# Loading q and k of later tiles in 32x32 blocks and transposing them on VectorE, in a chunked attention with a low-rank mixer and an MLP

## The chip, the cores and the metric

The kernel runs on one core of a Trainium2 chip. The metric is the device time of one execution in microseconds (us), the median of several runs; less is better. Engine names are those of the profile: PE is TensorE's matmul, PEld its weight load, DVE is VectorE, ACT is ScalarE, POOL is GpSimd, SP is SyncE. SP computes nothing here: it issues nearly all DMAs, one after the other. A row with "SPq" is such an issue.

## What is computed

The inputs are q, k and v of 8 batches, 8 heads, 576 rows and 64 columns, and the weights of a mixer (U, V) and of an MLP (w_ch1, w_ch2, 512 to 2048 to 512).

```python
def _attn_ref(q, k, v):                       # chunk = 64, nc = 9
    scores = scale * np.matmul(q_c, k_c.transpose(0, 1, 2, 4, 3))   # 64x64 a chunk and head
    scores = scores - np.max(scores, axis=-1, keepdims=True)
    attn = np.exp(scores)
    attn = attn / (np.sum(attn, axis=-1, keepdims=True) + 1e-09)
    return np.matmul(attn, v_c)               # back to B, H, S, D

def _moe_ref(x, U, V, w_ch1, w_ch2):          # x is batch, 576, 512
    h = x.transpose(0, 2, 1) @ U @ V          # rank 32, along the sequence
    u = x + h.transpose(0, 2, 1)
    return u + np.maximum(u @ w_ch1, 0.0) @ w_ch2
```

## The kernel before

**Tiling.** Batches are taken in four pairs (pair 0 to 3). The 1152 rows of a pair make nine tiles of 128 rows, written (pair, tile); tile 4 spans both batches. Three tiles make a group, so a pair has groups 0, 1 and 2.

**MLP.** For each group and each of the 16 blocks `f` of 128 hidden columns, `hidden` does twelve PE matmuls into `h` (L567; high and low parts of the data and the weights), ACT writes `hh` (`relu_high`, L575), DVE writes `hl` (`relu_low`, L580), and `project_out` does nine PE matmuls into three `o` banks (L593). These are 192 blocks. The `o` matmuls of a block stand on PE behind the `h` matmuls of the next one, so a block's `hh` and `hl` have the time of one set of `h` matmuls to become ready.

**Attention of a tile** (`attention_ops`). SP loads `qn`, `kn` and `vn` (`load_qk` L348 and L349, `load_v` L358). PE transposes q and k, four 128x128 blocks each, into a PSUM bank (`transpose`, L375); ACT copies the bank to SBUF as `qT_` and `kT_` (`evacuate`, L385). PE makes 32 small score matmuls for the tile's 64x64 blocks (L393), DVE takes maxima and subtracts (L407, L411), ACT exponentiates (L415), PE transposes the result (`eT_`) and multiplies with v (L424), DVE divides (L436 to L442). The tile's result `x` goes through the projection `y` (L495, L496), the low-rank addition (L523, L529), a transpose into `uth` and `utl` (L535 to L548), and then feeds the MLP of its group.

**Early and later tiles.** The nine tiles of pair 0 are "early" (`early`, L327): their q, k and v live in the weights' buffers, and the change leaves them alone. The 27 tiles of pairs 1 to 3 are later ones. Their `qn`, `kn`, `vn`, `qT_`, `kT_`, `ex`, `eT_` come from a pool of eight buffers of 128x512 (`slot`, L69); the SP issue that fills such a buffer waits until the work that last used it is done, and SP waits with it.

**Order.** The first part (pair 0's attention, the conversion of the weights, 32 MLP blocks, and tiles (1, 0) and (1, 1)) is put in order by a list planner written in the kernel (`order`, L124), from a cost in us, an engine and the buffers that each `Op` takes and frees. After that, `plan` (L744) hands the steps of attention, projection and mixing out evenly over the 16 blocks of a group: `attend` (L718) has for each tile a step that loads the next tile, then q, k, scores, and the transposed weights and values of the tile before. The framework's scheduler then fixes the row of instructions of each engine. Each engine works through its row strictly in order; a waiting instruction holds up all behind it. Every DMA on SP also waits for the landing of the DMA eight before it, since eight semaphores are used in turn.

Of the kernel before, what the change touches and what calls it, by code (L numbers as in the profile page):

```python
# [10 lines left out]
F32 = mybir.dt.float32  # L11
# [10 lines left out]
def kernel(  # L22
# [11 lines left out]
    nc = tc.nc  # L34
    B, H, S, D = q.shape
# [4 lines left out]
    P = 128  # L40
    C = 64
    D1 = D + 1
    HP = H // 2
    NCC = DM // P
    NF = DF // P
# [5 lines left out]
    XROOM = 3  # L51
    BLOCKS = [(hp, e, c) for hp in range(HP) for e in range(2) for c in range(2)]
    GN = GT * P
# [12 lines left out]
    def bank(name):  # L66
        return psum.tile([P, 512], F32, tag="bank", name=name)

    def slot(dtype, name, shape=(P, 512)):  # L69
        return work.tile(list(shape), dtype, tag="slot", name=name, bufs=NS)  # L70
# [33 lines left out]
    def wslot(shape, dtype, name):  # L104
        return wpool.tile([P, *shape], dtype, tag="w", name=name, bufs=NF)
# [214 lines left out]
    def segments(pr, t):  # L320
        lo, hi = t * P, (t + 1) * P
        for e in range(2):
            a, z = max(lo, e * S), min(hi, (e + 1) * S)
            if a < z:
                yield a - lo, z - a, 2 * pr + e, a - e * S

    def early(pr, t):  # L327
        return pr == 0 and t < NEARLY

    loaded = {}  # L330
    begun = {}
# [4 lines left out]
    def load_qk(pr, t):  # L336
        n = f"{pr}_{t}"
        if early(pr, t):
            words = wslot((4 * DM,), F32, "qkv_" + n)
            qn, kn = (words[:, z * DM : (z + 1) * DM].rearrange("p (h d) -> p h d", h=H) for z in range(2))  # L340
            vn = words[:, 2 * DM : 2 * DM + H * D1].rearrange("p (c a k) -> p c a k", c=2, k=D1)
        else:
            qn = slot(F32, "qn_" + n, (P, H, D))
            kn = slot(F32, "kn_" + n, (P, H, D))
            vn = slot(F32, "vn_" + n, (P, 2, HP, D1))
        nc.gpsimd.memset(vn[:, :, :, D:], 1.0)
        for r, m, b, s0 in segments(pr, t):
            nc.sync.dma_start(qn[r : r + m], q[b, :, s0 : s0 + m, :].rearrange("h s d -> s h d"))  # L348
            nc.sync.dma_start(kn[r : r + m], k[b, :, s0 : s0 + m, :].rearrange("h s d -> s h d"))  # L349
        loaded[pr, t] = qn, kn, vn  # L350

    def load_v(pr, t):
        vn = loaded[pr, t][2]
        for c in range(2):
            b, s0 = divmod(t * P + c * C, S)
            b += 2 * pr
            for e in range(2):
                (nc.gpsimd if early(pr, t) else nc.sync).dma_start(  # L358
                    vn[e * C : (e + 1) * C, c, :, 0:D],
                    v[b, e::2, s0 : s0 + C, :].rearrange("h s d -> s h d"),  # L360
                )

    def load(pr, t):
        load_qk(pr, t)
        load_v(pr, t)

    def attention_ops(pr, t, after=None):
        n = f"{pr}_{t}"
        st = {}
        mine = early(pr, t)  # L370

        def transpose(src, name):
            ps = st[name] = bank("ps_" + name + n)
            for j in range(4):
                nc.tensor.transpose(ps[:, j * P : (j + 1) * P], src[:, j * P : (j + 1) * P], ident)  # L375

        def evacuate(name):
            if name[0] == "e" or not mine:
                dst = slot(F32, name + n, (P, HP, P))
            elif name[0] == "q":  # L380
                st["qk"] = wslot((2, HP, P), F32, "qkT_" + n)
                dst = st["qk"][:, 0]
            else:
                dst = st["qk"][:, 1]
            nc.scalar.copy(dst.rearrange("p a b -> p (a b)"), st[name])  # L385
            st[name] = dst

        def scores():
            ps = [bank(f"sc{e}_{n}") for e in range(2)]
            for hp, e, c in BLOCKS:  # L390
# [8 lines left out]
                )  # L399
            st["sc"] = [p[:, 0 : HP * C].rearrange("p (h k) -> p h k", k=C) for p in ps]  # L400

        def maximum(e):
            if e == 0:
                st["ex"] = slot(F32, "ex_" + n, (P, HP, 2, C))
                st["mx"] = work.tile([P, 2, HP], F32, tag="mx", name="mx_" + n, bufs=2)
            mx = st["mx"][:, e, :]
            nc.vector.reduce_max(mx, st["sc"][e], axis=AX.X)  # L407

        def subtract(e):
            mx = st["mx"][:, e, :]  # L410
            nc.vector.tensor_sub(st["ex"][:, :, e, :], st["sc"][e], mx.unsqueeze(2).broadcast_to([P, HP, C]))  # L411
# [5 lines left out]
        def values():  # L417
# [3 lines left out]
            for hp, e, c in BLOCKS:  # L421
                rows = slice(e * C, (e + 1) * C)
                cs = slice(c * C, (c + 1) * C)
                nc.tensor.matmul(  # L424
                    ps[e][cs, hp * D1 : (hp + 1) * D1],
                    lhsT=st["eT_"][rows, hp, cs],
# [3 lines left out]
                )  # L430
            st["av"] = [p[:, 0 : HP * D1].rearrange("p (h k) -> p h k", k=D1) for p in ps]

# [6 lines left out]
        def scaled(e):  # L439
            if e == 0:  # L440
                st["x"] = work.tile([P, HP, 2, D], F32, tag="x", name="x_" + n, bufs=NX)
            nc.vector.tensor_mul(  # L442
                st["x"][:, :, e, :],
                st["av"][e][:, :, 0:D],
                st["sm"][:, e].unsqueeze(2).broadcast_to([P, HP, D]),
            )
            if e == 1:
                x_of[pr, t] = st["x"].rearrange("p a b k -> p (a b k)")

        src = lambda z: loaded[pr, t][z].rearrange("p h d -> p (h d)")  # L450
        flat = lambda: st["ex"].rearrange("p a b k -> p (a b k)")
        lq = Op("SP", 2.5, lambda: load_qk(pr, t), after, take="w" if mine else "slot slot slot", lat=2.2)
        lv = Op("POOL" if mine else "SP", 4.0 if mine else 2.5, lambda: load_v(pr, t), lq, lat=2.2)
        tq = Op("PE", 0.35, lambda: transpose(src(0), "qT_"), lq, begun.get((pr, t - 2)), take="bank")
        cq = Op("ACT", 0.58, lambda: evacuate("qT_"), tq, take="w" if mine else "slot", free="bank")
        tk = Op("PE", 0.35, lambda: transpose(src(1), "kT_"), lq, tq, take="bank")
        ck = Op("ACT", 0.58, lambda: evacuate("kT_"), tk, cq, take="" if mine else "slot", free="bank")
        sc = Op("PE", 0.62, scores, ck, take="bank bank", free="w" if mine else "slot slot slot slot")
        m0 = Op("DVE", 0.41, lambda: maximum(0), sc, take="slot mx")
        s0 = Op("DVE", 0.41, lambda: subtract(0), m0, free="bank")  # L460
        m1 = Op("DVE", 0.41, lambda: maximum(1), s0)
        s1 = Op("DVE", 0.41, lambda: subtract(1), m1, free="bank mx")
        ex = Op("ACT", 0.63, exp, s1)
        te = Op("PE", 0.35, lambda: transpose(flat(), "eT_"), ex, take="bank", free="slot")
        ce = Op("ACT", 0.58, lambda: evacuate("eT_"), te, take="slot", free="bank")
        av = Op("PE", 0.65, values, ce, lv, take="bank bank x", free="slot w" if mine else "slot slot")
        sm = Op("DVE", 0.5, sums, av, take="sm")
        x0 = Op("DVE", 0.415, lambda: scaled(0), sm, free="bank")
        x1 = Op("DVE", 0.415, lambda: scaled(1), x0, free="bank sm")
        begun[pr, t] = te  # L470
        return [[lq, lv], [tq, cq], [tk, ck], [sc, m0, s0, m1, s1, ex], [te, ce], [av, sm, x0, x1]]

    ybank = {}

# [182 lines left out]
    for item in LEAD.split():  # L657
        rank[0] += 1
        z, i = item[0], int(item[1:] or 0)
        if z == "U":  # L660
            u_done = u_ops()
        elif z == "V":
            v_done = v_ops()
        elif z == "W":
            w_done[i] = w_ops(i, w_done[i - 3][-1] if i > 2 else None)
        elif z == "T":
            xs[i] = attention_ops(0, i)[-1][-1]
        elif z == "P":
            ys[i] = project_ops(0, i, xs)[1]
        else:  # L670
            if i == 2:
                rank[0] = 0
            for t in range(GT * i, GT * i + GT):
                m = mix_ops(0, t, xs[t], ys, first=his.get(i))[1]
                his.setdefault(i, m[1])
                mixed.setdefault(i, []).append(m[2])
# [3 lines left out]
    for g, f0, f1 in STRETCHES:  # L680
        for f in range(f0, f1):
            rank[0] = BASE
            prev = block_ops(0, g, f, f == f0, f == f1 - 1, [*w_done[f], *mixed[g]], prev)
            blocks += 1
            if blocks in gates:
                rank[0] = 0
                attention_ops(1, gates[blocks], prev[0])
# [117 lines left out]
```

## Time and profile before

| | |
|---|---|
| median of 3 runs | 1030.82 us (1030.47 to 1032.12) |
| profiled execution, first to last instruction | 1032.0 us |
| ACT busy | 260.8 us (25%) |
| matmuls of the MLP: L567, L593 | 2304 and 1728 |
| SP issues of q and k of later tiles | 30 and 30, 256 KB each, 128 KB for tile 4 |
| SP issues of v of later tiles | 108, 64 KB each |

The profiled execution's span, 1032.0 us, is its own time; it is 1.2 us over the median. A matmul's "mean ns" is longer than the pace at which matmuls follow each other, since they are pipelined: the start times in the timeline tell the pace. In the source view, a row's three numbers are the shortest, the median and the longest duration in ns.

### The profile page before, as it was taken

The numbers are of one execution on the slowest core, as the hardware profiler recorded it, in microseconds if no ns is written. First come the engines' busy times: TensorE is split into PE (matmuls) and PEld (weight loads), VectorE is DVE, ScalarE is ACT, GpSimd is POOL, SyncE is SP. The second block draws the span as 40 slices with busy tenths as digits, with TensorE's granted clock in tenths as the row PEclk, the third lists the DMA queues.
The fourth block names the chain that finished last, engine by engine and source line by source line (L and its number), as shares of the span: only waits on it lengthen the run. The fifth ranks groups of instructions, "written<-read, shape, count | busy, mean of one in ns | idle before, by whom it ended". The sixth has DMA issues, their size and how long they took to land.

```text
span 1032.0 us, 16637 instructions
## 1 busy us (share of the span) xinstructions
PE 980.7 (95%) x7032; PEld 862.0 (84%) x7032; DVE 419.5 (41%) x834; ACT 260.8 (25%) x467; POOL 26.4 (3%) x78
## 2 busy tenths in 40 slices
PE   5486999999999999999999999999999999999998
PEld 4364888888888888988888888988888889999997
DVE  3498999973333342322423242322333332211211
ACT  3453234322322222222222222222222231111110
POOL 7100000000000000000000000000000000000000
PEclk9667899999999999999999999999999999999999
DMA  9952142305121211021021210111121000000000
GB/s 187 217 184 88 42 113 82 103 34 129 34 63 31 63 31 32 34 55 37 32 62 32 62 32 10 53 34 43 48 53 41 31 1 1 31 1 1 31 1 30
DMA packets 123157, 56.40 MB, mean 55 GB/s; under 512 B 107276, under 2 KB 115724, under 8 KB 123084
## 3 DMA queue, kind: packets, MB, share of 16 engines
q1 hardware_dynamic: 121932, 52.99, 20.1%
q0 software_dynamic: 1152, 2.36, 1.2%
q8 instruction: 55, 0.90, 0.4%
q14 instruction: 18, 0.15, 0.0%
HBM read 45.83 MB, written 9.51 MB: 54 GB/s over the span
## 4 chain that ended last, share of the span: by engine, by line
PE 69%; DVE 0%; ACT 0%; DVEq 0%; issue 0%; ACTq 0%
PE h L567 30%; PE o L593 30%; PE av L424 1%; PE sc L393 1%; PE ut L535 1%; PE ps_eT L375 1%; PE ps_kT L375 1%; PE ps_qT L375 1%; PE u L523 1%; PE y L496 1%; PE y L495 1%; DVE x L605 0%; DVE ex L411 0%; ACT ex L415 0%; DVEq L800 0%; DVE mx L407 0%
## 5 line engine op out<-in xcount | busy, mean ns | idle before, releaser
L567 PE MATMUL h<-uth,w 128*128 128x384 f32 x1536 | 427.1, 342 | 4.9 <-ACT w L308 2.1
L593 PE MATMUL o<-w,hh 128*128 128x512 f32 x1152 | 364.3, 403 | 0.6 <-ACT hh L575 0.6
L567 PEld LDWEIGHTS h<-uth,w 128*128 128x128 f32 x1536 | 282.4, 189 | 13.8 <-ACT w L308 2.6
L580 DVE SCALAR_TENSOR_TENSOR hl<-h,hh 128x384 fp32r<-128x384 f32 x192 | 106.8, 556 | 430.4 <-ACT hh L575 430.4
L567 PE MATMUL h<-utl,w 128*128 128x384 f32 x768 | 260.2, 339 | 0.4 <-DVE utl L548 0.4
L593 PEld LDWEIGHTS o<-w,hh 128*128 128x128 f32 x1152 | 207.8, 189 | 35.8 <-ACT hh L575 0.9
L593 PE MATMUL o<-w,hl 128*128 128x512 f32 x576 | 217.9, 395 | 0.0
L575 ACT ACTIVATE hh<-h 128x384 fp32r<-128x384 f32 x192 | 94.3, 491 | 477.3 <-PE h L567 477.2
L567 PEld LDWEIGHTS h<-utl,w 128*128 128x128 f32 x768 | 144.9, 189 | 6.6 <-DVE utl L548 0.6
L593 PEld LDWEIGHTS o<-w,hl 128*128 128x128 f32 x576 | 108.2, 188 | 25.0 <-DVE hl L580 0.3
L375 PE MATMUL ps_eT<-ident,ex 128*128 128x128 f32 x144 | 24.8, 301 | 25.0 <-ACT ex L415 25.0
L415 ACT ACTIVATE ex<-ex 128x512 f32<-128x512 f32 x36 | 22.7, 632 | 89.7 <-DVE ex L411 89.1
L375 PEld LDWEIGHTS ps_eT<-ident,ex 128*128 128x128 f32 x144 | 18.9, 153 | 31.1 <-ACT ex L415 27.9
L407 DVE TENSOR_REDUCE mx<-sc 128x4 f32<-128x256 f32 x72 | 28.0, 418 | 37.7 <-PE sc L393 37.7
L488 DVE TENSOR_TENSOR xl<-x,xh 128x512 fp32r<-128x512 f32 x40 | 27.2, 687 | 29.6 <-ACT xh L484 25.6
L529 DVE TENSOR_TENSOR x<-u,x 128x512 f32<-128x512 f32 x36 | 24.1, 684 | 26.7 <-PE u L523 26.4
L548 DVE TENSOR_TENSOR utl<-ut,uth 128x512 fp32r<-128x512 f32 x36 | 24.5, 690 | 25.2 <-ACT uth L543 25.1
L605 DVE TENSOR_TENSOR x<-o,x 128x512 f32<-128x512 f32 x48 | 31.2, 685 | 7.7 <-PE o L593 7.6
L543 ACT CAST uth<-ut 128x512 fp32r<-128x512 f32 x36 | 20.9, 587 | 40.4 <-PE ut L535 36.6
L385 ACT COPY eT<-ps_eT 128x512 f32<-128x512 f32 x36 | 21.1, 586 | 39.4 <-PE ps_eT L375 39.4
L484 ACT CAST xh<-x 128x512 fp32r<-128x512 f32 x40 | 24.1, 621 | 17.8 <-PE y L496 7.5
L411 DVE TENSOR_TENSOR ex<-sc,mx 128x256 f32<-128x256 f32 x72 | 28.0, 417 | 0.8
(74 smaller groups left out, 590.2 us busy)
## 6 DMA issues: line engine op xcount, KB each, us to landing
wraw<-in_moe_w_ch_dram SPq DMA_DIRECT2D x32, 512.0 KB, 4.5
out_dram<-x SPq DMA_DIRECT2D x36, 256.0 KB, 2.1
vn<-in_v_dram SPq DMA_DIRECT2D x108, 64.0 KB, 2.9
qn<-in_q_dram SPq DMA_DIRECT2D x24, 256.0 KB, 3.3
kn<-in_k_dram SPq DMA_DIRECT2D x24, 256.0 KB, 4.1
qkv<-in_v_dram POOLq DMA_DIRECT2D x36, 64.0 KB, 6.3
qkv<-in_q_dram SPq DMA_DIRECT2D x8, 256.0 KB, 9.4
qkv<-in_k_dram SPq DMA_DIRECT2D x8, 256.0 KB, 7.6
```

The lines of the kernel that those rows point to most:

```text
L375: nc.tensor.transpose(ps[:, j * P : (j + 1) * P], src[:, j * P : (j + 1) * P], ident)
L407: nc.vector.reduce_max(mx, st["sc"][e], axis=AX.X)
L411: nc.vector.tensor_sub(st["ex"][:, :, e, :], st["sc"][e], mx.unsqueeze(2).broadcast_to([P, HP, C]))
L484: nc.scalar.copy(st["h"], x_of[pr, i + 4 * e])
L488: nc.vector.tensor_sub(st["l"], x_of[pr, i + 4 * e], st["h"])
L529: nc.vector.tensor_add(x, st["u"], x)
L548: nc.vector.tensor_sub(ul[:, :, js], st["t"].rearrange("p (c t) -> p c t", c=NCC), uh[:, :, js])
L567: nc.tensor.matmul(ps[:, :GN], lhsT=w[:, z, cc], rhs=u[:, cc, :], start=(n == 0), stop=(n == 3 * NCC - 1))
L575: nc.scalar.activation(hh, ps[:, :GN], AF.Relu)
L580: nc.vector.scalar_tensor_tensor(hl, ps[:, :GN], 0.0, hh, op0=ALU.max, op1=ALU.subtract)
L593: nc.tensor.matmul(acc[j], lhsT=h[:, js], rhs=w2[f][:, z], start=(first and i == 0), stop=(final and i == 2),)
L605: nc.vector.tensor_add(x, ps, x)
```

## The change

Tiles of pairs 1 to 3 are loaded and transposed in another way. `qn` and `kn` become buffers of 128 partitions x 4 head pairs x 4 blocks x 32 columns. For each of q and k a tile is fetched by 16 DMAs (in tile 4, eight for each of its two halves): each brings one block of 32 rows and 32 of the 64 columns, for the four even or the four odd heads, to 32 partitions. That is 128 pieces of 128 bytes a DMA, 16 KB; before, it was one DMA of 128 rows and 8 heads, 1024 pieces of 256 bytes. One DVE instruction over the 128x512 buffer then transposes every 32x32 block and writes `qT_` or `kT_`, which have the layout that the scores read before. The eight PE transposes, the two PSUM banks and the two ACT copies of such a tile go away. The planner's costs for (1, 0) and (1, 1) have 0.6 us on DVE for each transpose.

```diff
+    TB = 32
...
-            qn = slot(F32, "qn_" + n, (P, H, D))
-            kn = slot(F32, "kn_" + n, (P, H, D))
+            qn = slot(F32, "qn_" + n, (P, HP, 4, TB))
+            kn = slot(F32, "kn_" + n, (P, HP, 4, TB))
...
         for r, m, b, s0 in segments(pr, t):
-            nc.sync.dma_start(qn[r : r + m], q[b, :, s0 : s0 + m, :].rearrange("h s d -> s h d"))
-            nc.sync.dma_start(kn[r : r + m], k[b, :, s0 : s0 + m, :].rearrange("h s d -> s h d"))
+            for dst, src in ((qn, q), (kn, k)):
+                if early(pr, t):
+                    nc.sync.dma_start(dst[r : r + m], src[b, :, s0 : s0 + m, :].rearrange("h s d -> s h d"))
+                    continue
+                for z in range(4):
+                    e, j = divmod(z, 2)
+                    for i in range(m // TB):
+                        s1 = s0 + i * TB
+                        nc.sync.dma_start(
+                            dst[z * TB : (z + 1) * TB, :, r // TB + i, :],
+                            src[b, e::2, s1 : s1 + TB, j * TB : (j + 1) * TB].rearrange("h t d -> t h d"),
+                        )
...
+        def turned(z, name):
+            dst = slot(F32, name + n, (P, HP, P))
+            nc.vector.transpose(dst.rearrange("p a b -> p (a b)"), loaded[pr, t][z].rearrange("p a i d -> p (a i d)"))
+            st[name] = dst
...
-        tq = Op("PE", 0.35, lambda: transpose(src(0), "qT_"), lq, begun.get((pr, t - 2)), take="bank")
-        cq = Op("ACT", 0.58, lambda: evacuate("qT_"), tq, take="w" if mine else "slot", free="bank")
-        tk = Op("PE", 0.35, lambda: transpose(src(1), "kT_"), lq, tq, take="bank")
-        ck = Op("ACT", 0.58, lambda: evacuate("kT_"), tk, cq, take="" if mine else "slot", free="bank")
+        if mine:
...
+        else:
+            cq = Op("DVE", 0.6, lambda: turned(0, "qT_"), lq, begun.get((pr, t - 2)), take="slot")
+            ck = Op("DVE", 0.6, lambda: turned(1, "kT_"), cq, take="slot")
+            turns = [[cq], [ck]]
...
-        return [[lq, lv], [tq, cq], [tk, ck], [sc, m0, s0, m1, s1, ex], [te, ce], [av, sm, x0, x1]]
+        return [[lq, lv], *turns, [sc, m0, s0, m1, s1, ex], [te, ce], [av, sm, x0, x1]]
```

Line numbers of the changed kernel are larger by one in its first part and by 22 in its last; the rows below have them as they are. The first two numbers in a name are pair and tile.

The row of SP before, from the loads of (1, 5) to those of (1, 7):

```order
L358 DMA vn_1_5_2516<-in_v_dram 64x4x64
L348 DMA qn_1_5_2514<-in_q_dram 128x8x64
L349 DMA kn_1_5_2515<-in_k_dram 128x8x64
L358 DMA vn_1_5_2516<-in_v_dram 64x4x64 x3
L358 DMA vn_1_6_2787<-in_v_dram 64x4x64
L348 DMA qn_1_6_2785<-in_q_dram 128x8x64
L358 DMA vn_1_6_2787<-in_v_dram 64x4x64
L349 DMA kn_1_6_2786<-in_k_dram 128x8x64
L358 DMA vn_1_6_2787<-in_v_dram 64x4x64 x2
L358 DMA vn_1_7_2868<-in_v_dram 64x4x64
L348 DMA qn_1_7_2866<-in_q_dram 128x8x64
```

and the same stretch of SP now:

```order
L357 DMA qn_1_5_2622<-in_q_dram 32x4x32 x16
L357 DMA kn_1_5_2623<-in_k_dram 32x4x32 x16
L369 DMA vn_1_5_2624<-in_v_dram 64x4x64 x4
L369 DMA vn_1_6_2915<-in_v_dram 64x4x64
L357 DMA qn_1_6_2913<-in_q_dram 32x4x32 x16
L357 DMA kn_1_6_2914<-in_k_dram 32x4x32 x16
L369 DMA vn_1_6_2915<-in_v_dram 64x4x64 x3
L357 DMA qn_1_7_3014<-in_q_dram 32x4x32 x16
L357 DMA kn_1_7_3015<-in_k_dram 32x4x32 x16
```

A tile's six issues are now 36, in the same queue and nearly the same sequence.

DVE before, at the end of group 2 of pair 0 (`hl_0_2_13` to `hl_0_2_15` belong to the last three blocks of that group; `x` is the low-rank addition, `utl` the low part of the next group's data):

```order
L580 SCALAR_TENSOR_TENSOR hl_0_2_13_3081<-h_0_2_13_3066,hh_0_2_13_3079 128x384
L529 TENSOR_TENSOR x_1_2_2463<-u_1_2_3095,x_1_2_2463 128x512
L548 TENSOR_TENSOR utl_1_0_3089<-ut_1_0_3083,uth_1_0_3088 128x4x128
L548 TENSOR_TENSOR utl_1_0_3089<-ut_1_1_3104,uth_1_0_3088 128x4x128
L580 SCALAR_TENSOR_TENSOR hl_0_2_14_3126<-h_0_2_14_3111,hh_0_2_14_3124 128x384
L548 TENSOR_TENSOR utl_1_0_3089<-ut_1_2_3128,uth_1_0_3088 128x4x128
L580 SCALAR_TENSOR_TENSOR hl_0_2_15_3159<-h_0_2_15_3144,hh_0_2_15_3157 128x384
```

and DVE there now:

```order
L602 SCALAR_TENSOR_TENSOR hl_0_2_13_3249<-h_0_2_13_3234,hh_0_2_13_3247 128x384
L463 STREAM_TRANSPOSE qT_1_7_3405<-qn_1_7_3014 128x512
L551 TENSOR_TENSOR x_1_2_2571<-u_1_2_3263,x_1_2_2571 128x512
L463 STREAM_TRANSPOSE kT_1_7_3429<-kn_1_7_3015 128x512
L570 TENSOR_TENSOR utl_1_0_3257<-ut_1_0_3251,uth_1_0_3256 128x4x128
L570 TENSOR_TENSOR utl_1_0_3257<-ut_1_1_3272,uth_1_0_3256 128x4x128
L602 SCALAR_TENSOR_TENSOR hl_0_2_14_3294<-h_0_2_14_3279,hh_0_2_14_3292 128x384
```

Both transposes of (1, 7) stand ahead of `hl_0_2_14`. Before, the PE transposes of that tile stood behind the `o` matmuls that read `hl_0_2_14`.

DVE before, where tile (1, 0) is transposed among the conversions of the weights (`wroom`, `wraw`, `w`):

```order
L101 TENSOR_TENSOR wroom_9_1410<-wroom_9_1410,wraw_9_1341 128x1024
L92 TENSOR_SCALAR wroom_10_1496<-wroom_10_1496 128x1024
L93 TENSOR_SCALAR wroom_10_1496<-wroom_10_1496 128x1024
L311 TENSOR_TENSOR w_9_1528<-wroom_9_1410,w_9_1528 128x1024
L580 SCALAR_TENSOR_TENSOR hl_0_1_6_1550<-h_0_1_6_1514,hh_0_1_6_1541 128x384
```

and now:

```order
L102 TENSOR_TENSOR wroom_9_1410<-wroom_9_1410,wraw_9_1341 128x1024
L93 TENSOR_SCALAR wroom_10_1526<-wroom_10_1526 128x1024
L463 STREAM_TRANSPOSE qT_1_0_1564<-qn_1_0_1488 128x512
L463 STREAM_TRANSPOSE kT_1_0_1566<-kn_1_0_1489 128x512
L312 TENSOR_TENSOR w_9_1558<-wroom_9_1410,w_9_1558 128x1024
L602 SCALAR_TENSOR_TENSOR hl_0_1_6_1584<-h_0_1_6_1544,hh_0_1_6_1581 128x384
```

The two transposes come in front of the last step of the weights of block 9 and of `hl_0_1_6`.

More of the change, by code (lines that the diff above doesn't have):

```diff
@@ L453, in attention_ops @@
         lv = Op("POOL" if mine else "SP", 4.0 if mine else 2.5, lambda: load_v(pr, t), lq, lat=2.2)
-        tq = Op("PE", 0.35, lambda: transpose(src(0), "qT_"), lq, begun.get((pr, t - 2)), take="bank")
-        cq = Op("ACT", 0.58, lambda: evacuate("qT_"), tq, take="w" if mine else "slot", free="bank")
-        tk = Op("PE", 0.35, lambda: transpose(src(1), "kT_"), lq, tq, take="bank")
-        ck = Op("ACT", 0.58, lambda: evacuate("kT_"), tk, cq, take="" if mine else "slot", free="bank")
+        if mine:
+            tq = Op("PE", 0.35, lambda: transpose(src(0), "qT_"), lq, begun.get((pr, t - 2)), take="bank")
+            cq = Op("ACT", 0.58, lambda: evacuate("qT_"), tq, take="w", free="bank")
+            tk = Op("PE", 0.35, lambda: transpose(src(1), "kT_"), lq, tq, take="bank")
+            ck = Op("ACT", 0.58, lambda: evacuate("kT_"), tk, cq, free="bank")
+            turns = [[tq, cq], [tk, ck]]
+        else:
+            cq = Op("DVE", 0.6, lambda: turned(0, "qT_"), lq, begun.get((pr, t - 2)), take="slot")
+            ck = Op("DVE", 0.6, lambda: turned(1, "kT_"), cq, take="slot")
+            turns = [[cq], [ck]]
         sc = Op("PE", 0.62, scores, ck, take="bank bank", free="w" if mine else "slot slot slot slot")
```

## The prediction, made before the changed kernel was run

> **What bounds the kernel now.** I read the page's busy shares and slices first, then the timeline of PE, then the groups by line.
>
> ```profile
> PE 980.7 (95%) x7032; PEld 862.0 (84%) x7032; DVE 419.5 (41%) x834; ACT 260.8 (25%) x467; POOL 26.4 (3%) x78
> PE   5486999999999999999999999999999999999998
> PEclk9667899999999999999999999999999999999999
> ```
>
> PE is full from about a tenth of the span on. Its pace shows in the start times: first a block of the MLP with nothing beside it, then one with both transposes of a tile.
>
> ```profile
> 1000.06 0.34 PE L567 MATMUL h<-utl,w 128*128 128x384 f32 x1
> ...
> 1004.27 0.34 PE L567 MATMUL h<-utl,w 128*128 128x384 f32 x1
> ```
>
> ```profile
> 521.22 0.34 PE L567 MATMUL h<-uth,w 128*128 128x384 f32 x1
> ...
> 523.33 0.61 PE L375 MATMUL ps_qT<-ident,qn 128*128 128x128 f32 x4
> ...
> 525.17 0.60 PE L375 MATMUL ps_kT<-ident,kn 128*128 128x128 f32 x4
> ...
> 526.32 0.34 PE L567 MATMUL h<-uth,w 128*128 128x384 f32 x1
> ```
>
> The plain block takes 1004.27 - 1000.06 = 4.21 us, the other 526.32 - 521.22 = 5.10. So a tile's eight transposes cost PE 0.89 us. DVE and ACT wait for PE most of the time:
>
> ```profile
> L580 DVE SCALAR_TENSOR_TENSOR hl<-h,hh 128x384 fp32r<-128x384 f32 x192 | 106.8, 556 | 430.4 <-ACT hh L575 430.4
> L385 ACT COPY kT<-ps_kT 128x512 f32<-128x512 f32 x27 | 15.9, 588 | 17.8 <-PE ps_kT L375 17.0 <-DMA kn<-in_k_dram 0.8
> ```
>
> The exception is the conversion of the weights, where DVE is full too (second column: DVE busy):
>
> ```profile
> 146.00:170.00 24.00, 23.28 (x29) 0.95 0.43 121
> 170.00:194.00 24.00, 22.10 (x34) 0.95 0.25 89
> 194.00:232.00 38.00, 30.98 (x57) 0.95 0.21 65
> ```
>
> **Removed.** From PE 27 x 0.89 = 24.0 us, all of it on the bound if nothing new is late. From ACT two copies a tile, 54 x 0.588 = 31.8 us, worth nothing: ACT waits for PE.
>
> **Added on DVE: 54 transposes of 128x512.** The trace has none. Its nearest rows are one-source and two-source operations of that size in SBUF:
>
> ```profile
> L93 DVE TENSOR_SCALAR wroom<-wroom 128x512 uint32<-128x512 uint32 x6 | 2.6, 428 | 0.2
> L101 DVE TENSOR_TENSOR wroom<-wroom,wraw 128x512 f32<-128x512 f32 x6 | 4.1, 690 | 0.2
> ```
>
> I take the dearer, 0.69 us, or 37 us in all (23 by the cheaper). Beside 430 us of waiting for hh this hides, except in the weights' stage.
>
> **Added on SP: 32 issues a tile in place of two.** This is where I expect the outcome to be decided. What an issue costs SP (shortest, median, longest ns), and the landing of vn:
>
> ```profile
> L348 SPq DMA_DIRECT2D qn<-in_q_dram x30: 373/542/1574, 146.0 to 785.1; - x30
> L358 SPq DMA_DIRECT2D vn<-in_v_dram x108: 595/614/2619, 147.4 to 790.9; - x108
> L608 SPq DMA_DIRECT2D out_dram<-x x36: 332/356/1000, 228.3 to 1028.9; - x36
> DMA to landing us min/median/max: 2.3/3.3/8.8
> ```
>
> A vn issue moves a quarter of the bytes of a qn issue and takes longer. Is it the shape? The halves of tile (1, 4), on 64 partitions as vn is, say so:
>
> ```profile
> 230.04 2.59 SPq L358 DMA_DIRECT2D vn<-in_v_dram  x4
> 232.73 0.55 SPq L348 DMA_DIRECT2D qn<-in_q_dram  x1
> ...
> 252.40 0.60 SPq L348 DMA_DIRECT2D qn<-in_q_dram  x1
> 253.05 0.63 SPq L349 DMA_DIRECT2D kn<-in_k_dram  x1
> ```
>
> Four vn issues take 2.59 us, 0.65 us from one to the next with the gap of 0.04 to 0.05; the half tiles' starts, 252.40 and 253.05, are 0.65 apart too. Only issues over 128 partitions come down to 0.37. The new ones cover 32. Bounds: 0.42 us a step (the shortest qn plus the gap) and, for a SP that is held up now and then as in the long rows, some 0.75. I take **0.65**, the row of the nearest shape; a byte count plays no visible part. Transfers are no limit: q1 below spent 20.1% of 16 engines' 1032 us on 121,932 packets, 27 ns each, so a tile's 4096 packets of q and k, even at the price of those of twice the size, take 4096 x 27 ns / 16 = 7 us of each engine. Eight DMAs in flight at 0.65 are 5.2 us, over the median landing of 3.3.
>
> ```profile
> q1 hardware_dynamic: 121932, 52.99, 20.1%
> ```
>
> A tile now keeps SP for 32 x 0.65 + 4 x 0.65 = 23.4 us. On average that fits: the stores and the 25 tiles loaded after 232 need some 600 us of the 800 left. But tiles (1, 2) to (1, 7) come close together. From the first load of (1, 2) at 232.73 to the landing of k of (1, 7), SP issues 6 x 32 = 192 blocks, 20 vn and 3 stores in a row: 192 x 0.65 + 20 x 0.65 + 3 x 0.42 + landing 2.3 = 141.4, so k lands at **374.1**. That holds if no wait for a buffer comes between; each first block waits for work on a tile loaded two before, which is long done when SP runs late. What waits for it:
>
> ```profile
> 323.24 1.28 DVE L548 TENSOR_TENSOR utl<-ut,uth 128x512 fp32r<-128x512 f32 x2
> 325.72 0.56 DVE L580 SCALAR_TENSOR_TENSOR hl<-h,hh 128x384 fp32r<-128x384 f32 x1 [1.20 <-ACT hh L575]
> ```
>
> ```profile
> 330.12 0.40 PE L593 MATMUL o<-w,hl 128*128 128x512 f32 x1
> ```
>
> The hl at 325.72 is `hl_0_2_14` (one utl pair behind the x that follows hl_0_2_13), and PE reads it at 330.12. In the changed row kT of (1, 7), two utl and that hl come in this sequence: k must land by 330.12 - 0.56 - 1.28 - 0.69 = 327.6. It is **46.5 us late**, and PE with it, since hl stands behind the transpose on DVE. The PE time saved on (1, 2) to (1, 6) is swallowed, since PE waits for SP there; that of (1, 0) and (1, 1) I leave out, as DVE is full there. Behind (1, 7) SP has room again. The tightest places are (2, 6), whose first q issue waits for a projection, then (2, 7):
>
> ```profile
> 517.21 0.48 SPq L348 DMA_DIRECT2D qn<-in_q_dram  x1
> ...
> 565.43 0.39 PE L593 MATMUL o<-w,hl 128*128 128x512 f32 x1
> ```
>
> Two tiles' blocks and four vn from 517.21, plus landing, are 517.21 + 41.6 + 2.6 + 2.3 = 563.7; the hl behind the transpose of (2, 7) is read at 565.43, less 0.56 and 0.69 is 564.2. That is even, so I take nothing for it, nor for (3, 7), where the pattern returns. From (1, 7) on 20 tiles keep their gain: 20 x 0.89 = 17.8.
>
> Tile (1, 0) has a smaller wait of the same kind.
>
> ```profile
> 145.99 0.43 SPq L348 DMA_DIRECT2D qn<-in_q_dram  x1
> ...
> 162.36 0.69 DVE L92 TENSOR_SCALAR wroom<-wroom 128x1024 f32<-128x1024 f32 x1
> ```
>
> Its k lands at 145.99 + 20.8 + 2.3 = 169.1; DVE comes to it when L92 is done and qT made, 163.05 + 0.69 = 163.7. Of 5.4 us of waiting and 1.4 of transposes, on an engine that idles 2 us in the next 24 and 7 in the 38 after, I let 4 through (0 to 6.8). The loads of the weights of block 12, queued behind, start 13.7 us later and still land before their turn.
>
> Last, PE slows down after a long wait. Four transposes behind 7.13 us of idling take 1.12 us, warm ones 0.61:
>
> ```profile
> 29.47 1.12 PE L375 MATMUL ps_eT<-ident,ex 128*128 128x128 f32 x4 [7.13 <-ACT ex L415]
> ...
> 38.45 0.61 PE L375 MATMUL ps_qT<-ident,qkv 128*128 128x128 f32 x4
> ```
>
> Within the stretch that SP sets it costs nothing more, behind its last wait some 2 us.
>
> **Sum.** 1032.0 + 46.5 + 4 + 2 - 17.8 = 1066.7 in the profile's time; less the 1.2 by which its span lies over the median, **1065**.
>
> **Rivals.**
> - *Issues cost what the cheapest qn does*, 0.42 a step. (1, 7)'s k lands at 232.73 + 80.6 + 13 + 1.3 + 2.3 = 329.9, 2.3 late, (1, 0) waits for nothing, and the kernel is faster: 1032.0 + 2.3 + 0.7 - 17.8 - 1.2 = **1016**. For it speak the 0.37 rows, against it that all of them have 128 partitions. The fixed parts of the chain, 232.73 + 13 + 1.3 + 2.3, are 249.3; the point that decides is the step at which 192 steps + 249.3 - 327.6, plus the 1 to 6 us of the small terms, equals 17.8: about 0.48 us.
> - *Everything hides*, 1032.0 - 24.0 - 1.2 = **1007**. This needs steps below (327.6 - 4.5 - 249.3) / 192 = 0.38, less than any load row with its gap. The Trainium skill, "DMA: Bandwidth & Descriptors", section "Issuing engines are not separate DMA queues", calls the sequencer's time to initiate a DMA "usually small relative to the DMA itself"; by that rule this rival would hold. The trace agrees for a single load (0.54 against 3.3 to landing), but not for 36 in a row on one queue.
> - *Issues are dearer or get held up*, 0.75 a step. (1, 7) is 65.7 late, and now pairs 2 and 3 stall too: from the release of (2, 3) at 441.5, 160 steps, 16 vn, stores and landing end at 575.5, 11.3 after 564.2, once a pair: 1032.0 + 65.7 + 22.6 + 6 - 17.8 - 1.2 = **1107**. For it: longest issues of 1.5 to 2.6 us, and a shape never seen.
>
> ```profile
> 441.52 0.39 SPq L348 DMA_DIRECT2D qn<-in_q_dram  x1
> ```
>
> **How the numbers follow.** Steps of 0.55 to 0.71, around the forecast: 0.62. The first rival 0.16, the second 0.05, the third 0.12, steps near the point of no change 0.05. The range takes in the first rival and reaches to steps of about 0.71: 1013 to 1095, with some 0.15 left outside. By over 0.2% (about what a measurement here can tell): faster 0.21, within 0.04, slower 0.75.
>
> **What would show it.** In the changed profile: block issues of 32 partitions at 595 to 615 ns, back to back from 233 to about 400 with hardly a gap; DVE idle before the transposes with the DMA as its releaser, in the main on (1, 3) to (1, 7), about 45 us in all, and PE idle for hl there; a clock below full in those slices; blocks of 4.21 us without transposes; DVE transposes of 0.43 to 0.69. Issues of 0.37 would prove it wrong at its root; so would SP waiting for buffers rather than DVE for DMAs, or a scheduler's row that lets hl pass.

## The result, and the profile after

| | before | changed |
|---|---|---|
| median of five runs, us | 1032.12 (1030.47 to 1032.71) | 1040.34 (1037.32 to 1045.58) |
| profiled execution's span, us | 1032.0 | 1040.8 |

The ratio is 1.0084, with a 95% interval of 1.0057 to 1.0111. The kernel became slower, as forecast, but by 8 us, where 33 were forecast.

The page of the changed kernel, with the rows that answer to those shown of before:

```profile
PE 968.5 (93%) x6816; PEld 845.7 (81%) x6816; DVE 452.9 (44%) x888; ACT 231.1 (22%) x413; POOL 26.6 (3%) x78
PE   5486999999588999999999999999999999999998
PEclk9678999999888999999999999999999999999999
q1 hardware_dynamic: 190092, 53.05, 22.7%
PE 76%; SPq 4%; DVE 3%; issue 2%; ACT 1%; DMA 1%; DVEq 0%; ACTq 0%
```

PE has 12 us less to do, and still the kernel ends later: slices 11 to 13 (260 to 338 us) are no longer full. SP's queue, whose share of the chain of work that ended last stands in the last line, is on the path with 4%, some 40 us.

What SP does there stands in its timeline (start, duration, operation, how many in a row):

```profile
232.75 9.05 SPq L357 DMA_DIRECT2D qn<-in_q_dram  x16
241.90 7.49 SPq L357 DMA_DIRECT2D kn<-in_k_dram  x16
249.80 2.59 SPq L369 DMA_DIRECT2D vn<-in_v_dram  x4
252.49 1.52 SPq L630 DMA_DIRECT2D out_dram<-x  x3
254.10 8.40 SPq L357 DMA_DIRECT2D qn<-in_q_dram  x16
262.61 7.48 SPq L357 DMA_DIRECT2D kn<-in_k_dram  x16
...
320.86 7.50 SPq L357 DMA_DIRECT2D kn<-in_k_dram  x16
...
330.43 8.40 SPq L357 DMA_DIRECT2D qn<-in_q_dram  x16
338.94 7.51 SPq L357 DMA_DIRECT2D kn<-in_k_dram  x16
346.49 3.35 SPq L369 DMA_DIRECT2D vn<-in_v_dram  x5
```

SP issues without a pause of over 0.42 us from the first block of (1, 2) to the last of k of (1, 7), as forecast. Sixteen blocks that nothing holds up take 7.5 us, 0.47 us a step. Over the whole stretch, 346.45 - 232.75 = 113.7 us less 20 vn at 0.65 and the stores' 1.6 leaves 99.1 us for 192 blocks: **0.52 us a step**, with all that held them up. The forecast had 0.65. The block issues themselves have a median of 0.43 us, where 0.595 to 0.615 were forecast.

Who waits for it shows in the timeline of all engines around (1, 3), and at the longest wait, around (1, 4):

```profile
261.10 0.86 PE L615 MATMUL o<-w,hl 128*128 128x512 f32 x3
264.19 0.71 DVE L463 STREAM_TRANSPOSE qT<-qn 128x512 f32<-128x512 f32 x1 [5.69 <-DMA kn<-in_k_dram]
264.94 0.59 ACT L396 COPY eT<-ps_eT 128x512 f32<-128x512 f32 x1 [7.03 <-DMA kn<-in_k_dram]
265.62 1.29 PE L435 MATMUL av<-vn,eT 64*64 64x65 f32 x32 [3.67 <-issue]
...
267.33 0.52 PE L589 MATMUL h<-utl,w 128*128 128x384 f32 x1
...
272.00 0.71 DVE L463 STREAM_TRANSPOSE kT<-kn 128x512 f32<-128x512 f32 x1 [5.04 <-DMA kn<-in_k_dram]
272.63 0.12 DVE L447 TENSOR_SCALAR sm<-av 128x4 f32<-128x4 f32 x1
272.76 0.69 PE L404 MATMUL sc<-kT,qT 64*64 64x64 f32 x32 [1.71 <-DVE sm L447]
...
287.21 0.71 DVE L463 STREAM_TRANSPOSE qT<-qn 128x512 f32<-128x512 f32 x1 [9.94 <-DMA kn<-in_k_dram]
287.96 0.59 ACT L396 COPY eT<-ps_eT 128x512 f32<-128x512 f32 x1 [11.28 <-DMA kn<-in_k_dram]
288.64 1.26 PE L435 MATMUL av<-vn,eT 64*64 64x65 f32 x32 [8.07 <-issue]
...
323.12 0.59 ACT L396 COPY eT<-ps_eT 128x512 f32<-128x512 f32 x1 [2.52 <-DVE qT L463]
```

DVE stands before both transposes until their blocks land. The wait is for the last block to be issued: seven transposes of (1, 3), (1, 4), (1, 6) and (1, 7) wait for over 1 us, and each starts 1.96 to 2.34 us after the start of its last block's issue, while a block's median time from issue to landing is 1.8. PE then idles, but not for hl. It idles for `sc` of (1, 3), which starts 0.05 us after its kT is made (the row names the tiny `sm`, which began 0.08 us before the transpose's end; `sc` does not read it). And it idles for `av` of (1, 2): its eT is copied by ACT only from 264.94, 0.04 us after qT of (1, 3) ends. The eT at 287.96 likewise starts 0.04 us behind the next qT, and the one at 323.12 has qT named as its releaser. All tiles share the pool of eight buffers; that these eT are written into the buffer which qT still reads is inferred, since the profile has no buffer numbers. So a late q of one tile also holds the `av` of the tile before it. Between 232 and 350 us PE idles for over 0.3 us six times, 20.4 us in all, each time before `sc` or `av`; in the kernel before it does so nowhere in that stretch. The next h matmuls are slow, 0.52 against 0.34 us.

The stage with its PE time (length, busy time of PE, PEld, DVE, ACT and POOL, granted clock, DMA share, GB/s), before and then after:

```profile
232.00:312.00 80.00, 79.72 (x731) 68.94 (x730) 26.79 (x71) 22.50 (x42) 0.68 (x6) 0.95 0.32 73
```

```profile
232.00:312.00 80.00, 63.72 (x526) 55.00 (x525) 26.59 (x64) 13.48 (x25) 0.45 (x4) 0.91 0.27 52
312.00:420.00 108.00, 103.32 (x737) 89.64 (x736) 40.81 (x88) 21.53 (x40) 0.45 (x4) 0.97 0.24 46
```

PE loses 16 us of busy time in the first stretch and 4 in the second (there it had 107.72 before). DVE is at a third of its time, and the DMA engines carry less than before, so neither is full.

The waits of the transposes, and the end of the wait that counts, in the timeline of DVE and then PE:

```profile
322.38 0.71 DVE L463 STREAM_TRANSPOSE qT<-qn 128x512 f32<-128x512 f32 x1 [1.18 <-DMA kn<-in_k_dram]
329.95 0.71 DVE L463 STREAM_TRANSPOSE kT<-kn 128x512 f32<-128x512 f32 x1 [5.21 <-DMA kn<-in_k_dram]
...
348.19 0.71 DVE L463 STREAM_TRANSPOSE kT<-kn 128x512 f32<-128x512 f32 x1 [2.22 <-DMA kn<-in_k_dram]
```

```profile
330.72 1.14 PE L404 MATMUL sc<-kT,qT 64*64 64x64 f32 x32 [3.77 <-DVE sm L447]
...
380.46 0.44 PE L589 MATMUL h<-uth,w 128*128 128x384 f32 x1
...
1008.54 0.34 PE L589 MATMUL h<-utl,w 128*128 128x384 f32 x1
```

and the PE rows of before that answer to the last two:

```profile
357.44 0.34 PE L567 MATMUL h<-uth,w 128*128 128x384 f32 x1
...
1000.06 0.34 PE L567 MATMUL h<-utl,w 128*128 128x384 f32 x1
```

Behind kT of (1, 6), at 330.72, PE waits for no load any more. The lateness of each of the 192 blocks of the MLP, its start in this trace against its start in the one before, is -0.9 us at block 32 (243.83 us), before PE first idles, and stands at **22.4 us** from block 44 to block 46. (Block 53 reads 380.46 - 357.44 = 23.0, but in `turns_alone`, below, that one block is 2 us up on its neighbours too.) From there it falls, to 20.5 at block 61, 14.2 at block 109, and 1008.54 - 1000.06 = **8.5** at the end. So the loss is made once, in 110 us, and the transposes that PE is spared in the 20 tiles afterwards win back 13.9 of it, 0.70 each.

### The profile page after: what moved, and what is told of

It is laid out like the page before. It is cut to its first block, busy times and chain, and to the rows that moved or that the text cites. A ratio compares the mean times of both kernels' runs of the same rounds, so it can differ in the third digit from the quotient of the medians.

```text
span 1040.8 us, 17210 instructions
## 1 busy us (share of the span) xinstructions
PE 968.5 (93%) x6816; PEld 845.7 (81%) x6816; DVE 452.9 (44%) x888; ACT 231.1 (22%) x413; POOL 26.6 (3%) x78
## 3 DMA queue, kind: packets, MB, share of 16 engines
q1 hardware_dynamic: 190092, 53.05, 22.7%
q0 software_dynamic: 1152, 2.36, 1.2%
## 4 chain that ended last, share of the span: by engine, by line
PE 76%; SPq 4%; DVE 3%; issue 2%; ACT 1%; DMA 1%; DVEq 0%; ACTq 0%
PE h L589 35%; PE o L615 34%; SPq L357 4%; PE sc L404 2%; PE av L435 1%; PE ps_eT L386 1%; PE ut L557 1%; PE u L545 1%; PE y L517 1%; PE y L518 1%; DMA kn<-in_k_dram 1%; DVE wraw L101 0%; DVE wroom L102 0%; DVE hl L602 0%; SPq L369 0%
## 5 line engine op out<-in xcount | busy, mean ns | idle before, releaser
L615 PE MATMUL o<-w,hh 128*128 128x512 f32 x1152 | 357.9, 401 | 0.8 <-ACT hh L597 0.6
L615 PEld LDWEIGHTS o<-w,hh 128*128 128x128 f32 x1152 | 210.9, 189 | 39.6 <-ACT hh L597 2.7
L418 DVE TENSOR_REDUCE mx<-sc 128x4 f32<-128x256 f32 x72 | 28.0, 418 | 34.7 <-PE sc L404 34.6
L510 DVE TENSOR_TENSOR xl<-x,xh 128x512 fp32r<-128x512 f32 x40 | 27.2, 687 | 27.3 <-ACT xh L506 23.3
L435 PEld LDWEIGHTS av<-vn,eT 64*64 64x64 f32 x864 | 16.5, 140 | 21.5 <-issue 21.3
L435 PE MATMUL av<-vn,eT 64*64 64x65 f32 x864 | 20.4, 231 | 12.7 <-issue 12.5
L404 PEld LDWEIGHTS sc<-kT,qT 64*64 64x64 f32 x864 | 16.0, 137 | 18.1 <-issue 9.1
```

The source lines that it names most:

```text
L404: nc.tensor.matmul(ps[e][cs, hp * C : (hp + 1) * C], lhsT=st["qT_"][rows, hp, cs], rhs=st["kT_"][rows, hp, cs], start=True, stop=True,)
L435: nc.tensor.matmul(ps[e][cs, hp * D1 : (hp + 1) * D1], lhsT=st["eT_"][rows, hp, cs], rhs=vn[rows, c, hp, :], start=True, stop=True,)
L510: nc.vector.tensor_sub(st["l"], x_of[pr, i + 4 * e], st["h"])
L615: nc.tensor.matmul(acc[j], lhsT=h[:, js], rhs=w2[f][:, z], start=(first and i == 0), stop=(final and i == 2),)
```

## The experiments

The theory is that SP's row of issues makes the loss: the wait of the transposes is a wait for the last block to be *issued*. Its rivals are the place of the transposes on DVE (ahead of hl, maximum, and the rest, they cost the same with any load), the transfers (twice as many pieces of half the size), and a loss that is spread over all tiles.

### Each half of the change alone

`loads_alone` is the kernel before with the 32 block loads of the change, into the old layout; PE still transposes and ACT copies.

```diff
-            nc.sync.dma_start(qn[r : r + m], q[b, :, s0 : s0 + m, :].rearrange("h s d -> s h d"))
-            nc.sync.dma_start(kn[r : r + m], k[b, :, s0 : s0 + m, :].rearrange("h s d -> s h d"))
+            for dst, src in ((qn, q), (kn, k)):
...
+                for z in range(4):
+                    e, j = divmod(z, 2)
+                    for i in range(m // 32):
+                        s1 = s0 + i * 32
+                        nc.sync.dma_start(
+                            dst[r + i * 32 : r + (i + 1) * 32, e::2, j * 32 : (j + 1) * 32],
+                            src[b, e::2, s1 : s1 + 32, j * 32 : (j + 1) * 32].rearrange("h t d -> t h d"),
+                        )
```

> The kernel before with the change's loads alone: q and k of later tiles come in 32 block issues a tile into the old layout; PE still transposes, ACT still copies. Theory SP (SP's row of issues from (1, 2) to (1, 8), 23 us late at its worst in the changed kernel, is the whole loss): that lateness stays and nothing is gained, 1050 to 1062 us, with PE waiting for k or q of (1, 3) to (1, 8) in its transposes. Rival DVE place (the loss comes from the transposes standing ahead of hl in DVE's row): no DVE transposes here, so 1031 to 1034.

Measured: 1056.37 us (1053.78 to 1058.07), ratio 1.0231 (1.0210 to 1.0252). The loads alone cost 24 us. The windows of this kernel and the timeline of PE:

```profile
232.00:312.00 80.00, 63.83 (x508) 54.82 (x507) 20.79 (x54) 16.47 (x31) 0.34 (x3) 0.91 0.27 52
```

```profile
260.68 1.09 PE L385 MATMUL ps_qT<-ident,qn 128*128 128x128 f32 x4 [6.02 <-DMA kn<-in_k_dram]
...
282.72 1.09 PE L385 MATMUL ps_qT<-ident,qn 128*128 128x128 f32 x4 [4.41 <-DMA qn<-in_q_dram]
```

PE loses 16 us in the same stretch as in the change, with no transpose on DVE at all; here it waits for the blocks itself. The lateness grows from -3.6 us at block 32 to 19.9 at block 43 and then stays within 1.3 us of that, since nothing is won back. That is 23.5 us lost in the dense stretch; in the change it was 23.3, from -0.9 to 22.4.

`turns_alone` keeps the DVE transposes of the change and loads q and k with one DMA each per segment. It transposes blocks that stand in other places than the reference needs, so its output is not the reference's; its instructions are those of the change but for the loads.

```diff
-                for z in range(4):
...
-                        nc.sync.dma_start(
-                            dst[z * TB : (z + 1) * TB, :, r // TB + i, :],
-                            src[b, e::2, s1 : s1 + TB, j * TB : (j + 1) * TB].rearrange("h t d -> t h d"),
-                        )
+                nc.sync.dma_start(
+                    dst.rearrange("p a i d -> p (a i d)")[r : r + m].rearrange("p (h d) -> p h d", h=H),
+                    src[b, :, s0 : s0 + m, :].rearrange("h s d -> s h d"),
+                )
```

> The changed kernel with the two large loads a tile of before; the DVE transposes stay where they are. The blocks are then not the ones that the scores want, so the numbers are others than the reference's; the work and its sizes are the same. Theory SP: 27 tiles keep their gain of 0.70 to 0.89 us and nothing is late, 1008 to 1014 us. Rival DVE place: as slow as the changed kernel, 1036 to 1044.

Measured: 1012.00 us (1011.27 to 1013.09), ratio 0.9804 (0.9788 to 0.9820).

```profile
232.00:312.00 80.00, 79.41 (x710) 68.11 (x711) 36.97 (x90) 17.88 (x33) 0.79 (x7) 1.00 0.35 80
```

PE is full again. That the DVE transposes stay where they are, as the expectation says, did not hold throughout: the scheduler puts at least one transpose of 17 of the 27 tiles one to seven instructions further forward in DVE's row. But those of (1, 3), (1, 4) and (1, 6), at which PE idled for 18.0 of the 20.4 us, stand in the same places, and here PE never idles for over 0.3 us between 230 and 420 us. With `loads_alone`, which has no transposes on DVE and loses as much, and `three_plain` below, in which the other 24 tiles' transposes stand as in the change, the place on DVE is dead as the cause of the loss. The move of the transposes by itself is worth 20 us, 0.74 for each of 27 tiles. The halves give -20 and +24; the change loses 8 rather than 4, since the 4.2 us that `turns_alone` gains from block 32 to block 44 are not had in the change, where PE waits instead.

### The queue, not the transfer

`k_on_pool` has the same 32 DMAs a tile, but GpSimd issues the 16 of k.

```diff
-                        nc.sync.dma_start(
+                        (nc.sync if dst is qn else nc.gpsimd).dma_start(
```

> The changed kernel with the 16 block loads of k of each later tile issued from GpSimd instead of SP; q and v stay on SP. Same pieces, same bytes, same DVE row. Theory SP: a tile keeps SP for 16 x 0.5 + 2.6 = 10.6 us, GpSimd for 16 x 0.65 = 10.4 beside it, (1, 7) is on time, 1010 to 1019 us. Rival transfer (pieces of 128 bytes keep the DMA engines or their landing busy): the same engines move the same pieces, 1036 to 1044. Rival DVE place: 1036 to 1044.

Measured: 1019.65 us (1017.92 to 1020.09), ratio 0.9872 (0.9853 to 0.9891). The same bytes issued from two queues are 21 us faster than from one. The pieces are not carried the same way, though:

```profile
q1 hardware_dynamic: 127884, 45.94, 18.5%
q0 software_dynamic: 14976, 9.47, 5.0%
```

In the change q1 has 190,092 packets and q0 1,152: a k DMA makes 144 packets when SP issues it and 32 when GpSimd does. So this run alone does not rule the transfer out. But the engines are busy as long (23.5% of this span, 23.9% in the change), and a k block takes 2.1 us to land instead of 1.8, so the gain is not a faster transfer. GpSimd's issues take longer than SP's 0.43:

```profile
L357 POOL DMA_DIRECT2D kn<-in_k_dram x432: 548/551/988, 95.8 to 784.6; - x144
```

The result is just past the upper end of what was expected (1019), and 7.7 us above `turns_alone`. By the starts of the MLP blocks most of that, 6.8 us, is lost between blocks 33 and 40, around (1, 2) to (1, 4); PE is busy for 74.79 of 80 us in the stretch 232 to 312. DVE still waits there for q of (1, 3) and (1, 4), 0.9 and 2.4 us, and the scheduler has put kT of (1, 3), (1, 4) and (1, 6) four or five instructions further back in DVE's row; how the 6.8 us divide between the two is not shown.

`halved` cuts every block load in two, by head pairs: 64 issues a tile, the same bytes in the same 128-byte pieces. One run.

```diff
...
+                        for g in range(2):
+                            nc.sync.dma_start(
+                                dst[z * TB : (z + 1) * TB, 2 * g : 2 * g + 2, r // TB + i, :],
+                                src[b, 4 * g + e : 4 * g + 4 : 2, s1 : s1 + TB, j * TB : (j + 1) * TB].rearrange("h t d -> t h d"),
+                            )
```

> The changed kernel with each block load cut in two (two heads each): 64 issues a tile, the same pieces of 128 bytes, the same bytes. Theory SP: at 0.47 us a step a tile takes 33 us of SP, so SP paces the whole kernel from 233 on, 25 tiles x 33 + 233 + 220 = 1260 to 1290 us; at 0.36, if smaller issues are cheaper, 1080 to 1130. Rival transfer: nothing changes, 1036 to 1046.

Measured: 1317.05 us. Each issue's cost did not fall with its bytes (shortest, median, longest ns), and DVE now waits for k on 23 tiles of 27 (total, times, longest us):

```profile
L358 SPq DMA_DIRECT2D qn<-in_q_dram x864: 311/425/1927, 144.7 to 1099.8; - x173
```

```profile
DVE kT L464 <- DMA kn<-in_k_dram: 202.9, 23, 14.4
```

It is above what either theory gave, but SP does pace the kernel: from 247 us on it issues without a pause to the last k at 1114.9. Of the 970 us from the first block at 144.7 to that one, 855 go to the 1728 blocks, 0.495 us each, 71 to 105 vn, 15 to 24 stores, and the rest to the weights' loads. The expected 1260 to 1290 had a step of 0.47 and no stores. The pieces are the same 128 bytes, and the transfer theory gave at most 14 us of this loss of 285 against the kernel before.

### Where the loss is made

`pair1_plain` leaves the nine tiles of pair 1 as before; `three_plain` only (1, 2), (1, 3) and (1, 4).

```diff
+    def plain(pr, t):
+        return pr == 1
...
-                if early(pr, t):
+                if early(pr, t) or plain(pr, t):
...
+        elif plain(pr, t):
+            tq = Op("PE", 0.35, lambda: transpose(src(0), "qT_"), lq, begun.get((pr, t - 2)), take="bank")
...
```

```diff
-        return pr == 1
+        return pr == 1 and 2 <= t <= 4
```

> The changed kernel with pair 1's nine tiles loaded and transposed as before; pairs 2 and 3 as in the change. Theory SP: only (1, 2) to (1, 8) stand so close that SP falls behind, so 18 tiles gain 0.70 to 0.75 us each and nothing is lost, 1017 to 1021 us. If the loss were spread over all later tiles (DVE place, transfer), two thirds of it would be left: 1036 to 1039.

> The changed kernel with tiles (1, 2), (1, 3) and (1, 4) alone loaded and transposed as before. Theory SP: the backlog that builds up over these three is gone; (1, 5) to (1, 8) have room for 18 us of SP each, and 24 tiles gain 0.70 to 0.75 us, 1013 to 1018 us. If SP falls behind on (1, 5) to (1, 8) all the same, 1020 to 1030; if the loss is spread over all tiles, 1036 to 1040.

Measured: 1020.49 us (1016.81 to 1021.22), ratio 0.9878 (0.9856 to 0.9901), and 1017.36 us (1016.58 to 1018.15), ratio 0.9859 (0.9841 to 0.9877). A loss spread over all tiles would have left two thirds of it or more. With three tiles of 27 undone the kernel is 23 us faster than the change: those three made the row too long, and the other 24, whose transposes stand in DVE's row as in the change, keep a gain. 24 x 0.74 = 17.8 would give 1014; 3 us of it are not had.

`three_plain_pool` joins the two remedies: the three tiles as before, and k's blocks of the other 24 issued by GpSimd.

> The same three tiles as before, and for the other 24 k's blocks from GpSimd. The version that should be fastest: the transposes alone took 1012, less three tiles' gain of 2.1 us, 1012 to 1016. If SP is no bound any more in three_plain, no faster than that.

Measured: 1016.38 us (1015.99 to 1016.74), ratio 0.9849 (0.9834 to 0.9863). That is just past the 1016 expected. It computes what the reference does and beats both kernels, by 1.5% and 2.3%; `three_plain`, a smaller edit, is within 0.1% of it.

```profile
232.00:312.00 80.00, 79.42 (x722) 68.19 (x721) 30.79 (x77) 20.72 (x38) 26.73 (x55) 1.00 0.34 72
```

### What an issue costs, by shape

`shapes` is the kernel before, with loads behind the last tile's that nothing reads: pieces of 32 words for four heads over 128, 64, 32 and 16 partitions (full, half, quarter, eighth), and of 64 words over 64 and 32 (wide). One run, 1033.96 us.

```diff
+    probe("full", 128, 32, 8)
+    probe("half", 64, 32, 8)
+    probe("quarter", 32, 32, 8)
...
+    probe("widehalf", 64, 64, 4)
+    probe("widequarter", 32, 64, 8)
```

> The kernel before with rows of loads added behind its last tile, that nothing reads: 8 each over 128, 64, 32 and 16 partitions of 4 x 32 numbers, and 4 over 64 and 8 over 32 partitions of 4 x 64. It measures the step by shape; the time stays within 1030 to 1036. If the step goes with the partitions: 32 at 0.47 and below, 64 at 0.65 in both widths, 128 at 0.42 to 0.58. If it goes with the number of pieces an issue describes (512, 256, 128, 64): falling in that sequence, and 64 x 4 x 64 like 64 x 4 x 32.

Shortest, median and longest ns of an issue on SP:

```profile
L780 SPq DMA_DIRECT2D full<-in_q_dram x8: 391/502/512, 852.8 to 856.5; - x8
L780 SPq DMA_DIRECT2D half<-in_q_dram x8: 601/614/616, 857.1 to 861.7; - x8
L780 SPq DMA_DIRECT2D quarter<-in_q_dram x8: 425/430/555, 862.5 to 865.9; - x8
L780 SPq DMA_DIRECT2D eighth<-in_q_dram x8: 423/424/430, 866.4 to 869.7; - x8
L780 SPq DMA_DIRECT2D widequarter<-in_q_dram x8: 430/430/1418, 872.8 to 877.2; - x8
...
L780 SPq DMA_DIRECT2D widehalf<-in_q_dram x4: 601/614/615, 870.1 to 872.1; - x4
```

The cost goes with the number of partitions, but not in their order: 64 are dear by themselves, at 0.61 in both widths; 32 and 16 stand at 0.43 and 0.42, 128 at 0.50 in a row. With the gap of 0.044 to the next issue that is 0.47, 0.66 and 0.55 a step for 32, 64 and 128, as the first expectation had them. The second, that it falls with the pieces, is wrong; so is the reason for which the forecast chose its step, that 64 partitions are nearer to 32 than 128 are.

## Why the prediction came out as it did

The mechanism is in the main the one forecast: SP's row of issues is too long for the dense stretch, and the transposes on DVE wait for it. The failed step is a term of the sum: **"It is 46.5 us late"**. It measured 22.4 us, and was mis-sized through the step of 0.65, "the row of the nearest shape", which measured 0.52. The terms against what the traces show, in us:

| term | forecast | measured |
|---|---|---|
| lateness out of the dense stretch, with PE's slow restart | 46.5 + 2 | 22.4 |
| wait at (1, 0) | 4 | none on DVE |
| won back by the later tiles | -17.8 | -13.9 |
| sum | +34.7 | +8.5 |
| time against before, by the spans | | +8.8 |

- **The step of an issue.** It was taken from vn and from the halves of a split tile, both over 64 partitions, as nearer to 32 than 128. `shapes` shows that 64 is the exception and no bound for 32; of the two bounds given, 0.42 was the near one (0.47 undisturbed). The step of 0.52 put into the forecast's own formula gives 192 x 0.52 + 249.3 - 327.6 = 21.5 us of lateness, and with the other terms unchanged 1032.0 + 21.5 + 4 + 2 - 17.8 - 1.2 = 1040.5. That this meets the measured 1040.34 is in part luck: the 4 us at (1, 0) did not occur, and the later tiles won back 3.9 us less. So it is with the point of no change, about 0.48: with no small terms and 13.9 won back the formula gives 0.48 again. By it the undisturbed issues alone would have come out near even, and the holds (single issues of up to 1.8 us) put the kernel on the slower side.
- **SP's row and its place.** Right: a row without a pause from 232.75, and the loss in (1, 2) to (1, 6). k of (1, 7) was transposed from 348.2, 20.6 after the 327.6 at which it was needed.
- **What waits.** Right to DVE, wrong on PE. PE did not wait for hl behind the transposes but for `sc` and, through ACT's eT, for `av`. The last wait that counted was on kT of (1, 6), 22.4 us late; (1, 7), itself 20.6 late, then held PE no more. The two differ by 2 us, so the sum hardly felt it. DVE idled 35 us before transposes with a DMA as the releaser, of 45 forecast:

```profile
L463 DVE STREAM_TRANSPOSE qT<-qn 128x512 f32<-128x512 f32 x27 | 19.0, 705 | 19.9 <-DMA kn<-in_k_dram 16.8 <-DMA qn<-in_q_dram 3.0
L463 DVE STREAM_TRANSPOSE kT<-kn 128x512 f32<-128x512 f32 x27 | 18.6, 690 | 15.4 <-DMA kn<-in_k_dram 14.4 <-DMA qn<-in_q_dram 0.9
```

- **The transposes on DVE.** Right: 0.70 us each, 0.69 taken, and hidden (`turns_alone`).
- **The gain per tile.** 0.89 was one block against one other; over a pair's nine tiles, blocks 62 to 110, PE's time fell from 239.56 to 233.24 us, 0.70 a tile, and `turns_alone` gives 0.74. The block that was read holds nothing but its MLP matmuls and the eight transposes; what takes back the other 0.19 a tile is not shown.
- **(1, 0).** Its blocks needed less time than forecast for the same reason as the rest, and had landed when DVE came to them (163.54 for q, 164.17 for k, both without a wait); the 4 us did not occur.
- **Pairs 2 and 3.** Even, as forecast; no wait of weight there.
- **The clock.** It was 0.91 in the stretch in which PE idles, below the 0.97 of the next, as forecast. But the kernel before shows 0.95 in its own full slices, so this sign says little.
- **The rivals.** The cheapest qn's step, 0.42, was nearer to the 0.47 of an undisturbed row than 0.65 was, but left no room for the holds. Steps of 0.75 were not seen, nor the second stall that they would have made. "Everything hides" needed a step below 0.38 and fell. The Trainium skill says in "DMA: Bandwidth & Descriptors", section "Issuing engines are not separate DMA queues", that the time to initiate a DMA is usually small beside the DMA itself. That holds for one load here (0.43 us against 1.8 to landing), and not for a row of 36 on one queue, which `halved` shows most plainly.

Left open: what single issues of 0.65 to 1.8 us wait for (7 of the 192, all of them of q), the 7 us that `k_on_pool` still loses, and the 3 us by which `three_plain` misses 24 full gains.

## What to carry to other kernels

Before replacing one large DMA by many small ones, multiply their number by the issue step of their own shape and hold that against the densest stretch of loads, not against the average of the run: 18 us of issuing a tile was nearly free in 24 of 27 tiles, and in the other three it made the row too long, which cost 23 us. Measure the step for the very shape, with a few loads behind the end of the kernel; the step taken from the nearest shape in the trace, 0.65, was a quarter above the 0.52 that the kernel needed. Where the move itself pays, as the transposes did, leave the few tiles of the dense stretch as they were, or spread their issues over a second queue.

## What the runs showed of the hardware

- On SP an issue of four heads' f32 over 64 partitions takes 0.61 us, dearer than one over 128 (0.50), 32 (0.43) or 16 (0.42); at 64 and at 32 twice the width costs the same (`shapes`).
- A k block of 16 KB makes 144 packets on SP's queue and 32 on GpSimd's, and lands in 1.8 and 2.1 us (the change, `k_on_pool`).
- Four PE transposes behind a wait of 4.4 us or 6.0 us take 1.09 us, against 0.61 warm, and the h matmuls behind 3.7 us of idling 0.52 against 0.34.
- The granted clock in a profile is no measure of time by itself here: from 420 to 1030 us the kernel before shows 0.95 and `shapes`, which is that kernel with some loads added, 1.00, and both take as long (1032.0 and 1032.1 us of span):

```profile
420.00:1030.00 610.00, 607.37 (x4097) 538.70 (x4095) 170.63 (x368) 126.88 (x239) 1.68 (x15) 0.95 0.12 30
```

```profile
420.00:1030.00 610.00, 606.77 (x4098) 538.08 (x4096) 170.57 (x368) 126.86 (x240) 1.68 (x15) 1.00 0.14 33
```

The first row is that of before, the second that of `shapes` (length, PE, PEld, DVE, ACT, POOL, granted clock, DMA share, GB/s).
